# Sliding-window attention in key blocks of 64: both products of the attention on smaller tiles of the array

## The chip, the cores and the metric

The kernel runs on one NeuronCore of a Trainium2 chip. The metric is device time in microseconds from the start to the end of one execution; lower is better. The core has a matrix engine (TensorE, PE in the profile), a vector engine (VectorE, DVE), an activation engine (ScalarE, ACT), a general engine (GpSimd, POOL), and a queue engine that issues DMA transfers (SyncE, SP). Matmuls write to PSUM, which the kernel uses as eight banks of 128 partitions by 512 float32 columns. [...]

## The reference

One layer on x of 2048 tokens by 576 features, all in bfloat16:

```
xn = layernorm(x)
q, k, v = split(xn @ wqkv)           # 32 heads of 18
p = softmax(q k^T / sqrt(18)), masked to 0 <= query - key < 256
s = (p v) @ wo
h = sigmoid(xn @ w_gate) * (xn @ w_up)      # 4608 wide
out = x + s * silu(h @ w_down)
```

A query sees its own key and the 255 before it. In blocks of 128 keys, a block of 128 queries meets three key blocks, the first and last of which are cut by a triangular mask. In blocks of 64 it meets five, of which the first and the last are cut.

## The kernel before

The 2048 tokens go through in four chunks of 512 (`NCH` = 4, variable `c`). For each chunk the program builds, in this order: layer norm; the projections to q, k and v (`project`, L451); the attention; the projection by `wo` (L717); the first half of the feed-forward network, FFN1, which computes gate and up (L760), and the second half, FFN2, the product with `w_down` (L834, and L864 for the last block). Every piece of work is an `Op` with an engine, an estimated duration, dependencies and PSUM banks to choose from. `schedule` places all ops by a list scheduler with these estimates and priorities, picks the banks, and writes out one fixed program for each engine; `emit` adds the semaphore waits. At run time every engine works strictly through its program, so an instruction whose input is late holds up all that stands behind it. The order of each engine is therefore known from the code alone.

The 32 heads lie in eight groups of four (`NHG`, variable `hg`). Head j of a group lies on partitions 32j to 32j+17 of `qkp`, so the four heads of a group can be multiplied at once.

- **Scores** (`build_unit`, L568). One unit makes up to 512 score columns for each of four heads. A matmul takes 128 keys of one head as weights, on a tile of 32 rows by 128 columns of the array, and 128 to 384 queries as the moving side. The four heads sit on four row tiles and write to PSUM banks 0, 1, 2 and 3. A unit holds all four banks. Then two ACT instructions take the exponential of two banks each (L591) into one of five buffers `expr`, and DVE multiplies the triangular masks `m13` on the blocks that are cut (L623). In chunks 1 to 3 a head group has three units of 512 columns; in chunk 0 two head groups share five units, 18 key-query blocks in all.
- **p times v** (`build_pv`, L651). Weights are 128 keys by 32 columns of v with a column of ones, on tiles of 128 rows by 32 columns, one column tile for each head; the moving side is `expr`. One head group writes one bank, taken from banks 4 to 7 (FFN1 takes its banks from the same four). The op is held in `pending` and put directly ahead of a later score unit as one op (`pvsc`), so that PE goes from p times v to scores without going back to the FFN.
- **After it** (`after_pv`): DVE transposes the bank in 32 by 32 blocks (L667), takes the reciprocal of the sums (L671), scales (L675) and transposes back (L681); DMAs (L208) put the heads' rows together in `oT` for `wo`.

The list scheduler sets the scores and p times v between stretches of FFN1, whose matmuls come in pairs: gate on the upper 64 rows of the array, up on the lower 64, at the same time. `SKEW` is the number of steps by which up runs behind gate, so that in each chunk the first `SKEW` gate steps and the last `SKEW` up steps have no partner. `FB_CUTS` says where an FFN1 op may be cut to let other work in. Weights of FFN1 are streamed again in each chunk through a ring of three buffers (`RW`).

PE has four forms of tile in this program: the whole array (FFN2, warm-up, transposes of chunk 0), 64 by 128 (FFN1, q/k/v, `wo`), 32 by 128 (scores) and 128 by 32 (p times v). The scheduler's estimate adds `MODE_NS` where the form changes.

Of the kernel before, what the change touches and what calls it, by code (L numbers as in the profile page):

```python
# [5 lines left out]
ALU = mybir.AluOpType  # L6
# [42 lines left out]
SKEW = 2  # L49
# [6 lines left out]
FB_CUTS = (0, 3, 7)  # L56
LAST = 448
W_GATE = 2

# [108 lines left out]
class Builder:  # L168
# [46 lines left out]
    def alloc_memory(self):  # L215
# [33 lines left out]
        self.m13 = sb("m13", [P, 2, P], bf16)  # L249
# [9 lines left out]
        self.psb = self.ps.bitcast(bf16)  # L259

# [4 lines left out]
    def build(self):  # L265
# [22 lines left out]
        for c in range(NCH):  # L288
# [18 lines left out]
    def build_init(self):  # L307
# [7 lines left out]
        m1 = op("POOL", 300, lambda e: e.memset(self.m13[:, :, :], 1.0), "m1", prio=1)  # L315
        m2 = op("POOL", 300, lambda e: e.affine_select(
            self.m13[:, 0, :], self.m13[:, 0, :], pattern=[[1, P]], compare_op=ALU.is_ge, fill=0.0,
            base=0, channel_multiplier=-1), "m2", deps=[m1], prio=1)
        self.op_mask = op("POOL", 300, lambda e: e.affine_select(
            self.m13[:, 1, :], self.m13[:, 1, :], pattern=[[-1, P]], compare_op=ALU.is_ge, fill=0.0,  # L320
            base=-1, channel_multiplier=1), "m3", deps=[m2], prio=1)
# [208 lines left out]
    def attn_steps(self, c):  # L530
        kb0 = c * QPC
        steps = []
        if c == 0:
            for a in range(0, NHG, 2):
                b = a + 1
                steps += [([(a, 0, 0, 3, 0), (a, 3, 3, 1, 3)], True), ([(a, 1, 1, 3, 0), (b, 3, 3, 1, 3)], False),
                          ([(a, 2, 2, 2, 0), (b, 2, 2, 2, 2)], False), (a, None), ([(b, 0, 0, 3, 0)], False),
                          ([(b, 1, 1, 3, 0)], True), (b, None)]
        else:
            for a in range(NHG):  # L540
                steps += [([(a, kb0, 0, 3, 0), (a, kb0 - 2, 0, 1, 3)], False),
                          ([(a, kb0 + 2, 2, 2, 0), (a, kb0 - 1, 0, 2, 2)], True),
                          ([(a, kb0 + 1, 1, 3, 0), (a, kb0 + 3, 3, 1, 3)], False), (a, None)]
        return steps

    def build_attn(self, c):
        self.where, self.masks, self.exps = {}, {}, {}
        for u, (what, merge) in enumerate(self.attn_steps(c)):
            if merge is None:
                self.build_pv(c, what)  # L550
            else:
                self.build_unit(c, u, what, merge)

    def build_unit(self, c, u, pieces, merge):
        kb0 = c * QPC
        where = self.where
        nblk = max(pos + n for (_, _, _, n, pos) in pieces)
        hgs = sorted({p[0] for p in pieces})
        es, de = self.r_exp.take()
        ps = Psum((0, 1, 2, 3))  # L560

        def f_sc(e):
            for hg, kb, q0, n, pos in pieces:
                for j in range(4):
                    r0 = 32 * j
                    b = ps.banks[j] * 512 + pos * P
                    k0 = CH + (kb - kb0) * P if kb >= kb0 else 2 * CH + (kb - kb0 + 2) * P
                    r = e.matmul(self.ps[:, b:b + n * P],  # L568
                                 self.qkp[r0:r0 + DH, hg, k0:k0 + P],
                                 self.qkp[r0:r0 + DH, hg, q0 * P:(q0 + n) * P],  # L570
                                 start=True, stop=True, tile_position=(r0, 0))
            return r
        deps = de + [self.op_tail[hg] for hg in hgs]
        for _, kb, q0, n, pos in pieces:
            deps += self.op_q[q0:q0 + n] + ([self.op_k[kb - kb0]] if kb >= kb0 else [])
        pend = self.pending if merge else None
        if pend:
            self.pending = None
            o = self.pe(pend[1] + MODE_NS + nblk * P / 2.4 + 30, lambda e, a=pend[0], b=f_sc: (a(e), b(e))[1],
                        f"pvsc:{c}:{hgs[0]}:{u}", deps=pend[2] + deps, prio=0, psum=[pend[3], ps], mode=("c32", "r32"))  # L580
            pend[4](o)
        else:
            o = self.pe(nblk * P / 2.4 + 30, f_sc, f"sc:{c}:{hgs[0]}:{u}", deps=deps, prio=1, psum=[ps], mode="r32")
# [3 lines left out]
        for pr in range(2):  # L587
            def f_ex(e, pr=pr):
                b = ps.banks[0] * 512
                src = self.ps[:, b:b + 2048].rearrange("p (b c) -> p b c", b=4)[:, 2 * pr:2 * pr + 2, 0:nblk * P]  # L590
                return e.activation(self.expr[:, es, 2 * pr:2 * pr + 2, 0:nblk * P], src, ACTF.Exp, scale=SM_SCALE)  # L591
            exps.append(self.rd("ACT", act_ns(2 * nblk * P), f_ex, f"ex:{c}:{hgs[0]}:{u}:{pr}", deps=[o], prio=1, psum=[ps]))
        spec = {}
        for hg, kb, q0, n, pos in pieces:
            for i in range(n):
                qi = q0 + i
                where[(hg, kb, qi)] = (es, pos + i)
                dlt = kb0 + qi - kb
                if dlt == 0:
                    spec[pos + i] = 0  # L600
# [542 lines left out]
```

## Time and profile before

| | before |
|---|---|
| median of 3 runs | 575.86 us (575.33 to 576.46) |
| profiled execution, span | 574.0 us |
| median less span | 1.9 us |
| mean granted TensorE clock | 0.999 |
| PE busy | 566.3 us, 99% |
| DVE busy | 293.9 us, 51% |
| ACT busy | 303.0 us, 53% |
| scores (L568), matmuls | 704 |
| p times v (L651), matmuls | 704 |

The span runs from the first to the last instruction of the profiled execution; its device time beyond the span is not given separately, and the difference to the median of the runs stands in for it. In the profile, L568 is line 568 of the kernel, `18*128 18x384` in a row of PE is a tile with 18 rows of weights by 128 columns and 384 moving columns, and PEld is the loading of weights, which the profile lists beside the matmuls. The ends of matmuls are modelled, so two rows of PE can overlap by their lengths; the starts are measured, and it is from start to start that durations on PE are read below. Releasers in brackets say what ended an idle time.

### The profile page before, as it was taken

To read this page: it belongs to the slowest core of one execution; us is meant where nothing else is said; L and a number is where in the kernel's file an instruction comes from. 1 tells how busy PE (TensorE), PEld (TensorE's weight loads), DVE (VectorE), ACT (ScalarE), POOL (GpSimd) and SP (SyncE) were. 2 spreads that over 40 slices of the span, in tenths; PEclk is the share of its full clock that TensorE was granted. 3 is DMA by queue.
4 is the path that set the end of the run, shared out by engine and by line. 5 is a ranking of instruction groups with operands and counts; after the bars stand their busy time and mean duration, and the time that the engine had idled before them with its cause. 6 is when DMAs were issued, how large, how long until landed. Compare 5 with 4: busy or idle time off the path is not lost.

```text
span 574.0 us, 14808 instructions
## 1 busy us (share of the span) xinstructions
PE 566.3 (99%) x6350; PEld 273.6 (48%) x6350; DVE 293.9 (51%) x589; ACT 303.0 (53%) x404; POOL 23.4 (4%) x51
## 2 busy tenths in 40 slices
PE   8999999999999999999999999999999999999996
PEld 5634443457444444455753444344654444444554
DVE  5147877422247886622115888672122676774112
ACT  7456777214448887420307787760242778872201
POOL 3001110000001100000000011000000000000000
PEclk9999999999999999999999999999999999999999
DMA  8999999436936665341893666414479356651010
GB/s 206 216 197 242 224 228 228 84 68 117 203 74 136 144 157 126 82 84 42 138 220 79 146 140 150 109 46 99 56 137 185 84 124 136 136 126 41 1 40 22
DMA packets 124861, 72.82 MB, mean 127 GB/s; under 512 B 53630, under 2 KB 124286, under 8 KB 124798
## 3 DMA queue, kind: packets, MB, share of 16 engines
q1 hardware_dynamic: 124798, 71.90, 58.5%
q8 instruction: 50, 0.82, 0.7%
q14 instruction: 13, 0.11, 0.1%
HBM read 55.22 MB, written 2.36 MB: 100 GB/s over the span
## 4 chain that ended last, share of the span: by engine, by line
PE 95%; SPq 2%; DMA 2%; issue 0%; DVE 0%; ACT 0%
PE ps L760 50%; PE ps L834 23%; PE ps L451 8%; PE ps L568 5%; PE ps L651 4%; PE ps L717 3%; SPq L208 2%; PE ps L864 2%; DMA wqkv_sb<-in_A_wqkv_dram 1%; DMA wgs<-in_B_w_up_dram 1%; DVE thf L897 0%; ACT thf L895 0%; DVE thf L899 0%; DVE xf L901 0%
## 5 line engine op out<-in xcount | busy, mean ns | idle before, releaser
L760 PE MATMUL ps<-xn,wgs 64*128 64x512 bf16 x2592 | 298.2, 377 | 1.2 <-DMA wgs<-in_B_w_up_dram 1.2
L591 ACT ACTIVATE expr<-ps 128x1024 bf16<-128x1024 f32 (+1 forms) x184 | 174.9, 1003 | 45.2 <-PE ps L568 45.2
L760 PEld LDWEIGHTS ps<-xn,wgs 64*128 64x128 bf16 x2592 | 118.6, 94 | 153.4 <-issue 18.7
L834 PE MATMUL ps<-wd_sb,hT 128*128 128x512 bf16 (+1 forms) x1080 | 135.0, 286 | 0.0
L746 ACT ACTIVATE tring<-ps 128x512 bf16<-128x512 f32 x144 | 86.3, 600 | 61.7 <-PE ps L760 60.3
L623 DVE TENSOR_TENSOR expr<-expr,m 128x1024 bf16<-128x1024 bf16 (+1 forms) x152 | 81.9, 572 | 67.8 <-ACT expr L591 67.7
L750 DVE SCALAR_TENSOR_TENSOR hT<-tring,ps 128x512 bf16<-128x512 bf16 x144 | 97.1, 675 | 35.3 <-ACT tring L746 28.6
L834 PEld LDWEIGHTS ps<-wd_sb,hT 128*128 128x128 bf16 x1080 | 68.0, 98 | 66.3 <-issue 3.1
L895 ACT ACTIVATE thf<-ps 128x576 bf16<-128x576 f32 (+2 forms) x17 | 10.6, 623 | 110.6 <-PE ps L834 102.8
L897 DVE SCALAR_TENSOR_TENSOR thf<-thf,ps 128x576 bf16<-128x576 bf16 (+2 forms) x17 | 12.2, 719 | 89.5 <-ACT thf L895 89.4
L451 PE MATMUL ps<-wqkv_sb,xn 64*128 64x288 bf16 x864 | 54.7, 283 | 0.4 <-ACT xn L440 0.3
L451 PEld LDWEIGHTS ps<-wqkv_sb,xn 64*128 64x128 bf16 x864 | 42.7, 94 | 11.5 <-issue 1.6
L568 PE MATMUL ps<-qkp 18*128 18x128 bf16 (+2 forms) x704 | 36.1, 275 | 0.0
L667 DVE STREAM_TRANSPOSE tf<-ps 128x512 f32<-128x512 f32 x32 | 22.8, 714 | 12.4 <-PE ps L568 10.9
L568 PEld LDWEIGHTS ps<-qkp 18*128 18x128 bf16 x704 | 10.8, 92 | 33.4 <-issue 20.3
L499 DVE CAST pk<-ps 128x576 bf16<-128x576 f32 x15 | 11.3, 756 | 27.8 <-PE ps L451 27.8
L651 PE MATMUL ps<-expr,vau 128*32 128x256 bf16 (+2 forms) x704 | 25.6, 277 | 0.0
L633 POOL COPY qkp<-qkp 128x256 bf16<-128x256 bf16 x24 | 11.6, 485 | 315.0 <-PE ps L568 315.0
L681 DVE STREAM_TRANSPOSE op__63<-pk 128x512 bf16<-128x512 bf16 x32 | 22.7, 709 | 1.1 <-DVE pk L675 0.2
L651 PEld LDWEIGHTS ps<-expr,vau 128*32 128x32 bf16 x704 | 13.1, 96 | 15.3 <-ACT tring L746 6.8
L717 PE MATMUL ps<-wo_sb,oT 64*128 64x512 bf16 (+1 forms) x288 | 19.2, 283 | 0.0
L500 ACT ACTIVATE pk<-ps 128x576 bf16<-128x576 f32 x12 | 7.8, 652 | 18.6 <-PE ps L451 18.6
(42 smaller groups left out, 148.6 us busy)
## 6 DMA issues: line engine op xcount, KB each, us to landing
wgs<-in_B_w_gate_dram SPq DMA_DIRECT2D x48, 240.0 KB, 3.8
wgs<-in_B_w_up_dram SPq DMA_DIRECT2D x48, 240.0 KB, 4.8
wgs<-in_B_w_up_dram SPq DMA_DIRECT2D x48, 192.0 KB, 4.1
wgs<-in_B_w_gate_dram SPq DMA_DIRECT2D x48, 192.0 KB, 4.7
wd_sb<-in_B_w_down_dram SPq DMA_DIRECT2D x9, 576.0 KB, 5.9
xf<-in_A_x_dram SPq DMA_DIRECT2D x18, 144.0 KB, 2.3
out_dram<-xf SPq DMA_DIRECT2D x15, 144.0 KB, 1.8
xr<-in_A_x_dram SPq DMA_DIRECT2D x14, 144.0 KB, 4.2
```

The lines of the kernel that those rows point to most:

```text
L451: r = e.matmul(self.bank(ps, HV, hf), self.xn[r0:r0 + 64, k, i * P:(i + 1) * P], self.wqkv_sb[r0:r0 + 64, j, k, :], start=(k == 0), stop=( ...
L568: r = e.matmul(self.ps[:, b:b + n * P], self.qkp[r0:r0 + DH, hg, k0:k0 + P], self.qkp[r0:r0 + DH, hg, q0 * P:(q0 + n) * P], start=True, st ...
L591: return e.activation(self.expr[:, es, 2 * pr:2 * pr + 2, 0:nblk * P], src, ACTF.Exp, scale=SM_SCALE)
L623: return e.tensor_tensor(ap, ap, m, ALU.mult)
L651: r = e.matmul(self.ps[32 * j:32 * j + 32, b + q0 * P:b + (q0 + n) * P], vf[:, v0:v0 + 32], self.expr[:, es, j, pos * P:(pos + n) * P], st ...
L667: t1 = self.rd("DVE", dve_ns(CH), lambda e, ps=ps: e.transpose(tf.rearrange("p g d -> p (g d)"), self.bank(ps)), f"t1:{c}:{hg}", deps=[o_p ...
L681: t2 = self.op("DVE", dve_ns(CH), lambda e, on=on: e.transpose(self.op_[:, hg % NOT, :], on.rearrange("p g d -> p (g d)")), f"t2:{c}:{hg}" ...
L717: r = e.matmul(self.bank(ps2[w], n1 - n0, n), self.oT[r0:r0 + 64, kt, qi * P:(qi + 1) * P], self.wo_sb[r0:r0 + 64, kt, n0:n1], start=(swap ...
L746: return e.activation(self.tring[:, st_, :], self.bank(ps), ACTF.Tanh, scale=0.5)
L750: return e.scalar_tensor_tensor(self.hT[:, ft, :], self.tring[:, st_, :], 1.0, self.bank(ps), ALU.add, ALU.mult)
L760: return e.matmul(self.bank((pg, pu)[gu][ft]), self.wgs[r0:r0 + 64, slots[ft // FG], i, fl * P:(fl + 1) * P], self.xn[r0:r0 + 64, i, :], s ...
L834: r = e.matmul(self.ps[:, b + n0:b + n1], lhsT, self.wd_sb[:, q, fl, n0:n1], start=(ft == 0), stop=(ft == NFT - 1))
```

## The change

The attention is cut into key blocks of 64 in place of 128.

- **Scores.** A matmul takes 64 keys as weights on a tile of 32 rows by 64 columns. Even key blocks go to the lower 64 output partitions and odd ones to the upper 64 (`low` and `up` in `build_unit`), so eight tiles are in the array. A unit is always 512 columns wide; `slots` orders its pieces by length, and the two halves of a unit may have pieces of unequal length. Two head groups together have five units in chunks 1 to 3 (one of them shared, `half`) and four in chunk 0. The matmuls of the scores go from 704 to 1472.
- **p times v.** The weights are 64 keys by 32 columns, on tiles of 64 rows by 32 columns; the upper and the lower half of the array take the odd and the even key blocks and sum into different banks. One op does two head groups and holds four banks, which are now banks 0 to 3 (`PVB`), the ones that the scores use. `pending` and `pvsc` are gone. The matmuls of p times v go from 704 to 1440.
- **After it.** For each head group DVE transposes two banks (`t1`, `t3`) and adds them (`ad`). Two of the three buffers `pk` serve as room for this; POOL sets them to zero again once in each chunk (`pkz`), before the next chunk's projections are written there.
- **Masks** of 64 by 64 (`m64`) on blocks of 64, 152 multiplications of mostly 512 columns.
- `SKEW` goes from 2 to 3, `FB_CUTS` to steps of three, and the last FFN2 block of chunks 0 to 2 may also take banks 4 to 7 (`F2B`).

```diff
-SKEW = 2
+SKEW = 3
...
-FB_CUTS = (0, 3, 7)
+FB_CUTS = (0,3,6)
...
+F2B = ((0, 1), (2, 3), (6, 7), (4, 5))
+PVB = ((0,), (1,), (2,), (3,))
...
+        self.pkf = self.pk.bitcast(f32)
...
+            self.op_pkz = [self.op("POOL", 2000, lambda e: e.memset(self.pk[:, 1:RPK, :, :], 0.0), f"pkz:{c}",
+                                   deps=self.op_on[c], prio=1)]
...
+        for a in range(0, NHG, 2):
+            b = a + 1
+            if c == 0:
+                for h in (a, b):
+                    steps += [("unit", [(h, 4, 4, 1, 0), (h, 0, 0, 5, 1), (h, 6, 6, 2, 6)],
+                               [(h, 1, 0, 6, 0), (h, 7, 7, 1, 7), (h, 7, 7, 1, 6)],
+                               [(0, P, 1, 5, 0), (0, P, 0, 6, (0,)), (64, P, 0, None, None)]),
+                              ("unit", [(h, 2, 2, 5, 0), (h, 4, 5, 3, 5)], [(h, 3, 3, 5, 0), (h, 5, 5, 3, 5)],
+                               [(0, P, 0, 4, 0), (64, P, 5, None, 0)])]
+                steps += [("pv", a)]
+                continue
+            half = [("unit", [(a, 4, 4, 4, 0), (b, 4, 4, 4, 4)], [(a, -1, 0, 4, 0), (b, -1, 0, 4, 4)],
+                     [(0, 64, 0, 4, (0,)), (64, P, 3, 7, (1,))])]
+            for h in (a, b):
+                steps += [("unit", [(h, 0, 0, 5, 0), (h, -2, 0, 3, 5)], [(h, 3, 3, 5, 0), (h, 5, 5, 3, 5)],
+                           [(0, P, 0, 4, 0), (0, P, 5, 7, 2)]),
+                          ("unit", [(h, 2, 2, 5, 0), (h, 6, 6, 2, 5), (h, -4, 0, 1, 7)],
+                           [(h, 1, 1, 5, 0), (h, 7, 7, 1, 5), (h, -3, 0, 2, 6)],
+                           [(0, P, 0, 4, 0), (0, P, 5, 7, 0)])] + half
+                half = []
+            steps += [("pv", a)]
...
+        slots = sorted(((-max(p[3] for p in low[k:k + 1] + up[k:k + 1]), k) for k in range(max(len(low), len(up)))))
 
         def f_sc(e):
-            for hg, kb, q0, n, pos in pieces:
+            for _, k in slots:
                 for j in range(4):
                     r0 = 32 * j
-                    b = ps.banks[j] * 512 + pos * P
-                    k0 = CH + (kb - kb0) * P if kb >= kb0 else 2 * CH + (kb - kb0 + 2) * P
-                    r = e.matmul(self.ps[:, b:b + n * P],
-                                 self.qkp[r0:r0 + DH, hg, k0:k0 + P],
-                                 self.qkp[r0:r0 + DH, hg, q0 * P:(q0 + n) * P],
-                                 start=True, stop=True, tile_position=(r0, 0))
+                    for half, pieces in enumerate((low, up)):
+                        if k >= len(pieces):
+                            continue
+                        hg, kb, q0, n, pos = pieces[k]
+                        b = ps.banks[j] * 512 + pos * 64
+                        k0 = CH + kb * 64 if kb >= 0 else 2 * CH + (kb + 4) * 64
+                        r = e.matmul(self.ps[64 * half:64 * half + 64, b:b + n * 64],
+                                     self.qkp[r0:r0 + DH, hg, k0:k0 + 64],
+                                     self.qkp[r0:r0 + DH, hg, q0 * 64:(q0 + n) * 64],
+                                     start=True, stop=True, tile_position=(r0, 64 * half))
             return r
...
+            self.runs.setdefault(hg, ([], []))[kb % 2].append((kb, q0, n, es, pos))
+        ns = 512 / 2.4 + 30
+        o = self.pe(ns, f_sc, f"sc:{c}:{hgs[0]}:{u}", deps=deps, prio=1, psum=[ps], mode="r32")
...
+        for p0, p1, pa, pb, kind in masks:
...
+            exps.append(self.op("DVE", dve_ns(512 if pb is not None else 256, 2.0), f_mk,
+                                f"mk:{c}:{hgs[0]}:{u}:{pa}", deps=(exps if kind is None else ex) + self.op_mask, prio=1))
...
-        ps = Psum((4,), (5,), (6,), (7,), *(((0,), (1,), (2,), (3,)) if hg == NHG - 1 else ()))
+        ps2 = {hg: [Psum(*PVB) for _ in range(2)] for hg in pair}
...
+        runs = {hg: [sorted(dict(((r[0], r[1]), r) for r in side).values(), key=lambda r: -r[2])
+                     for side in self.runs[hg]] for hg in pair}
+        ncol = sum(64 * max(sum(r[2] for r in side) for side in runs[hg]) for hg in pair)
+        used = sorted({r[3] for hg in pair for side in runs[hg] for r in side})
         def f_pv(e):
+            for hg in pair:
+                for m in range(max(len(side) for side in runs[hg])):
+                    for j in range(4):
+                        v0 = (hg * 4 + j) * (DH + 1)
+                        for half, side in enumerate(runs[hg]):
+                            if m >= len(side):
+                                continue
+                            kb, q0, n, es, pos = side[m]
+                            b = ps2[hg][half].banks[0] * 512
+                            p0 = 64 * half
+                            vf = self.vau[p0:p0 + 64, (kb0 + kb // 2) % NVB, :, :].rearrange("p h d -> p (h d)")
+                            r = e.matmul(self.ps[32 * j:32 * j + 32, b + q0 * 64:b + (q0 + n) * 64],
+                                         vf[:, v0:v0 + 32], self.expr[p0:p0 + 64, es, j, pos * 64:(pos + n) * 64],
+                                         start=(m == 0), stop=(m == len(side) - 1), tile_position=(p0, 32 * j),
+                                         skip_group_check=True)
             return r
-        self.pending = (f_pv, ncol / 2.4 + 30, deps, ps, lambda o: self.after_pv(c, hg, ps, o, used))
-        if hg == NHG - 1:
-            o = self.pe(ncol / 2.4 + 30, f_pv, f"pv:{c}:{hg}", deps=deps, prio=0, psum=[ps], mode="c32")
-            self.pending[4](o)
-            self.pending = None
...
+        o = self.pe(ncol / 2.4 + 30, f_pv, f"pv:{c}:{a}", deps=self.masks[a] + self.masks[a + 1] + vdeps, prio=0,
+                    psum=ps2[a] + ps2[a + 1], mode="c32")
+        for es in used:
+            self.r_exp.release(es, o)
+        mul = None
+        pkf = [self.pkf[:, k, :, :].rearrange("p h d -> p (h d)") for k in (1, 2)]
+        bufs = {a: (self.tf[:, :, :, :].rearrange("p a b d -> p (a b d)"), pkf[1]), a + 1: (pkf[0], pkf[1])}
+        ads = []
+        qk = self.op_q + self.op_k
+        for hg in pair:
+            tf, tg = bufs[hg]
+            t1 = self.rd("DVE", dve_ns(CH), lambda e, tf=tf, hg=hg: e.transpose(tf, self.bank(ps2[hg][0])),
+                         f"t1:{c}:{hg}", deps=[o, self.last_mul] + qk, prio=3, psum=ps2[hg][:1])
+            t3 = self.rd("DVE", dve_ns(CH), lambda e, tg=tg, hg=hg: e.transpose(tg, self.bank(ps2[hg][1])),
+                         f"t3:{c}:{hg}", deps=[o, self.last_mul] + qk + ads, prio=3, psum=ps2[hg][1:])
+            tf, tg = (t.rearrange("p (g d) -> p g d", d=32)[:, :, 0:DH + 1] for t in (tf, tg))
+            ads = [self.op("DVE", dve_ns(16 * (DH + 1)), lambda e, tf=tf, tg=tg: e.tensor_tensor(tf, tf, tg, ALU.add),
+                           f"ad:{c}:{hg}", deps=[t1, t3], prio=3)]
+            bufs[hg] = (tf, ads[0])
+        for hg in pair:
+            self.after_pv(c, hg, o, *bufs[hg])
...
-        on = self.pk[:, hg % RPK, (hg // RPK % 2) * 16:(hg // RPK % 2) * 16 + 16, :]
-        prev = self.op_on[c][hg - 2 * RPK] if hg >= 2 * RPK else None
+                     deps=[ad] + dr, prio=1)
+        on = self.pk[:, 0, hg % 2 * 16:hg % 2 * 16 + 16, :]
...
-            cands = ((0, 1), (2, 3)) if blocks[-1] == QPC - 1 else ((6, 7), (4, 5), (0, 1), (2, 3))
+            cands = F2B if blocks[-1] == QPC - 1 else ((6, 7), (4, 5), (0, 1), (2, 3))
```

More of the change, by code (lines that the diff above doesn't have):

```diff
@@ L589, in f_ex @@
                 b = ps.banks[0] * 512
[L590 to L600, printed above, removed]
-                elif dlt == 2:
-                    spec[pos + i] = 1
@@ L603, in build_unit @@
[L603 to L622 removed]
+                src = self.ps[:, b:b + 2048].rearrange("p (b c) -> p b c", b=4)[:, 2 * pr:2 * pr + 2, :]
```

136 lines of the change are left out of this document (47 added, 89 removed).

## The prediction

> **What bounds the kernel now.** I read the page first, for the busy time and the chain that ended last.
>
> ```profile
> span 574.0 us, 14808 instructions
> PE 566.3 (99%) x6350; PEld 273.6 (48%) x6350; DVE 293.9 (51%) x589; ACT 303.0 (53%) x404; POOL 23.4 (4%) x51
> PE 95%; SPq 2%; DMA 2%; issue 0%; DVE 0%; ACT 0%
> PE ps L760 50%; PE ps L834 23%; PE ps L451 8%; PE ps L568 5%; PE ps L651 4%; PE ps L717 3%; SPq L208 2%; PE ps L864 2%; DMA wqkv_sb<-in_A_wqkv_dram 1%; DMA wgs<-in_B_w_up_dram 1%; DVE thf L897 0%; ACT thf L895 0%; DVE thf L899 0%; DVE xf L901 0%
> ```
>
> PE carries 95% of the chain, and the attention's two lines (L568, L651) are 9% of the span on it. The waits of PE say whether it is really never held up.
>
> ```profile
> engine line waited for: us in total, times, longest us
> PE ps L760 <- DMA wgs<-in_B_w_up_dram: 1.2, 1, 1.2
> ```
>
> After its start PE waits once, 1.2 us in chunk 0. So a change of the attention is worth what it does to PE's own time, plus any wait it brings. PE's own time I took from the order in time, from start to start:
>
> ```profile
> start us, us, engine line op out<-in xcount [idle before <-releaser]
> 221.69 0.40 PE L568 MATMUL ps<-qkp 18*128 18x384 bf16 x8
> 222.02 2.76 PE L760 MATMUL ps<-xn,wgs 64*128 64x512 bf16 x24
> 224.72 0.40 PE L568 MATMUL ps<-qkp 18*128 18x384 bf16 x8
> 225.05 2.98 PE L760 MATMUL ps<-xn,wgs 64*128 64x512 bf16 x26
> 227.96 0.84 PE L651 MATMUL ps<-expr,vau 128*32 128x384 bf16 x24
> 228.73 0.40 PE L568 MATMUL ps<-qkp 18*128 18x256 bf16 x8
> 229.06 2.55 PE L760 MATMUL ps<-xn,wgs 64*128 64x512 bf16 x22
> ...
> 62.76 0.34 PE L568 MATMUL ps<-qkp 18*128 18x384 bf16 x4
> 63.03 2.98 PE L760 MATMUL ps<-xn,wgs 64*128 64x512 bf16 x26
> 65.94 0.67 PE L651 MATMUL ps<-expr,vau 128*32 128x384 bf16 x16
> 66.55 0.34 PE L568 MATMUL ps<-qkp 18*128 18x384 bf16 x4
> ...
> 162.51 2.11 PE L760 MATMUL ps<-xn,wgs 64*128 64x512 bf16 x16
> 164.56 0.40 PE L568 MATMUL ps<-qkp 18*128 18x384 bf16 x8
> ```
>
> From these rows come three prices.
> - FFN1: 26 matmuls take 2.91 us, 24 take 2.70, so 0.108 each, and 0.11 remains at the end of each stretch (2.70 - 24 x 0.108). Between forms of tile PE therefore loses about 0.11 us.
> - p times v: 1536 columns per tile take 0.77 us, the 1152 of chunk 0 take 0.61. That is 0.42 ns a column and 0.12 fixed. Scores: 512 columns 0.33, 384 columns 0.27, so 0.47 ns and 0.09. I use 0.43 ns a column, and 0.11 us for each change of form.
> - An FFN1 step without its partner: 16 matmuls, the first two alone, took 2.05 us, where 16 x 0.108 + 0.11 is 1.84. So 0.105 more for each.
>
> That several tiles do run at once shows in a window of 16 ns after the start of a unit and of a p times v:
>
> ```profile
> 221.69 0.34 PE L568 MATMUL ps<-qkp 18*128 18x384 bf16 x4
> 227.96 0.35 PE L651 MATMUL ps<-expr,vau 128*32 128x384 bf16 x4
> ```
>
> Four matmuls start within 16 ns, some 4 ns apart, on four row tiles as on four column tiles.
>
> **The change on PE, part by part.**
>
> *Columns.* Before: 45 blocks of 128 by 128 for each of eight groups, 46,080 columns for scores and as many for p times v. After, with eight tiles at once: in chunks 1 to 3 a pair of groups has three units of 512. Its other two units have pieces of 5, 2|1 and 1|2 blocks. PE starts matmuls in the order written, so I take each slot by its longer half, 5+2+2 = 9 blocks, 576 columns; that makes 2688 for the pair, 12 pairs. In chunk 0 a group has one unit of 512 and one with slots 1|6, 5|1, 2|1, which is 13 blocks or 832 columns and not 512; 2688 for a pair again, 4 pairs. Scores: 43,008. p times v: 20 blocks a group in chunks 1 to 3 (the halves match slot for slot), 17 in chunk 0: 12 x 2560 + 4 x 2176 = 39,424. Together 82,432 for 92,160: 9728 fewer x 0.43 ns = -4.2 us.
>
> *Changes of form.* Counted in the instruction order of PE, which is fixed without a run: 240 before, 206 after. 96 stretches of attention with 28 inner steps from p times v to scores become 92 stretches without; the cuts between FFN2 and 64-row work go from 20 to 22. -34 x 0.11 = -3.7 us.
>
> *SKEW.* One more step at each end of FFN1 is alone, in four chunks: 8 x 0.108 = +0.9 us.
>
> *Starting eight tiles.* At 4 ns each the last of eight starts 14 ns later than the last of four, and the drain waits for it: 92 stretches x 14 ns = +1.3 us.
>
> *Loading weights.* No row shows 64-column weights on eight tiles. Low end 0: the fixed prices of p times v (32-column weights, 0.12) and of scores (128 columns, 0.09) hardly differ, so width does not show. High end: one whole load at the start of each stretch. A load is recorded with under 0.1 us:
>
> ```profile
> L568 PEld LDWEIGHTS ps<-qkp 18*128 18x128 bf16 x704 | 10.8, 92 | 33.4 <-issue 20.3 <-ACT expr L591 7.2 <-ACT tring L746 5.9
> L591 ACT ACTIVATE expr<-ps 128x1024 bf16<-128x1024 f32 x168 | 162.8, 1021 | 41.9 <-PE ps L568 41.9
> L623 DVE TENSOR_TENSOR expr<-expr,m 128x512 bf16<-128x512 bf16 x64 | 26.5, 419 | 3.1 <-ACT expr L591 3.1
> ```
>
> 92 x 0.092 = 8.5 us. The trace lies near the low end; I take +1.0.
>
> [...]
>
> **What runs beside PE.** ACT loses work: 184 exponentials become 152 of 1.02 us. DVE gains 32 transposes and 32 additions and loses mask time (152 multiplications of mostly 512 columns at 0.42, 64 us for 87). In chunk 2 its load was
>
> ```profile
> core 0: us, PE busy (x) PEld busy (x) DVE busy (x) ACT busy (x) POOL busy (x), PEclk, DMA share, GB/s
> 300.00:384.00 84.00, 84.00 (x1006) 34.31 (x1006) 62.36 (x126) 63.90 (x82) 5.65 (x12) 1.00 0.51 118
> ```
>
> 74%, so there is room on average. What matters is one place: scores and p times v now share banks 0 to 3, so the first unit after a p times v waits for all four transposes. DVE's order there (pairs 1 and 3 of chunks 1 to 3) is transpose, transpose, FFN product, addition, transpose, reciprocal, product, scaling, transpose. Prices from start to start:
>
> ```profile
> 346.02 0.68 DVE L750 SCALAR_TENSOR_TENSOR hT<-tring,ps 128x512 bf16<-128x512 bf16 x1
> 346.62 0.71 DVE L667 STREAM_TRANSPOSE tf<-ps 128x512 f32<-128x512 f32 x1
> 347.25 0.17 DVE L398 BATCH_NORM_AGGREGATE mv<-bnst 128x2 f32<-128x12 f32 x1
> 347.36 0.25 DVE L671 RECIPROCAL rrec<-tf 128x16 f32<-128x16 f32 x1
> 347.53 0.10 DVE L401 TENSOR_SCALAR veps<-mv 128x1 f32<-128x1 f32 x1
> 347.65 0.46 DVE L675 TENSOR_TENSOR pk<-tf,rrec 128x288 bf16<-128x288 f32 x1
> 348.14 0.71 DVE L681 STREAM_TRANSPOSE op__63<-pk 128x512 bf16<-128x512 bf16 x1
> ```
>
> Three transposes at 0.63 and the last in full 0.71, two products at 0.60, reciprocal 0.17, scaling 0.49, addition about 0.47 (nearest row: scaling, 288 elements for 304): 4.9 us, some 5.1 with the signals. PE has 48 FFN1 matmuls there, 48 x 0.108 + 0.11 = 5.3. With pair 2 it is 42 (4.6 us), and reciprocal and last transpose come earlier, 4.0. In chunk 0 the third gap is 36 (4.0 us), about even. The cover is thin but there: +0.5 us for waits. If PE runs ahead of it, the next score unit is late, and the FFN1 behind it in the queue.
>
> ```profile
> 343.11 1.93 ACT L591 ACTIVATE expr<-ps 128x1024 bf16<-128x1024 f32 x2
> ```
>
> Ahead of p times v nothing gets worse: from its last unit PE has 30 FFN1 matmuls (3.3 us and the unit's 0.37), and the two exponentials (1.93), two masks and the signals need some 3.4.
>
> At the end of a chunk p times v now comes after the last FFN1, eight FFN2 matmuls into it, so the DMAs to `oT` meet the transposes of the next chunk's xn on SP:
>
> ```profile
> 248.49 11.56 SPq L207 DMA_TRANSPOSE xn<-xnr  x8
> 252.80 17.82 PE L834 MATMUL ps<-wd_sb,hT 128*128 128x512 bf16 x144
> 520.29 4.15 SPq L208 DMA_DIRECT2D oT<-op__63  x6
> ```
>
> DVE needs some 7 to 10 us for the pair (its xn normalisations stand in between), SP 11.6 + 4.2 plus two earlier transfers of 0.7 and the waits, about 19 us from the end of FFN1. PE has FFN2's 17.7 us, p times v 1.2, then the projections, whose first six read the first two token blocks, transposed ahead of that. Nothing waits. In chunk 3 `wo` stands 136 FFN2 matmuls (17 us) behind p times v; 6.1 us of DVE and 4.2 of SP leave over 6 for the landing. `pkz` on POOL is done in the same shadow. Without it a late xn would stop PE outright.
>
> **Sum.** 574.0 - 4.2 - 3.7 + 0.9 + 1.3 + 1.0 + 0.5 = 569.8 us span; with the 1.9 us by which the median exceeds the span, 571.7.
>
> **Rivals.**
> 1. *Eight tiles do not run at once*: the two halves of a row group take turns, or PE cannot start matmuls faster than it does per matmul now. For it: no row shows row and column tiles together. Against it: the two rows of four starts in 16 ns, one of them of four tiles over the same 128 rows. Both column sums come once more, 82,432 x 0.43 = 35 us: 607.
>    [...]
> 2. *Slower by the shared banks.* DVE comes to the transposes with FFN products and masks ahead of it, and PE stands at the first unit after p times v, in 11 places (the first gap of chunk 0, 72 matmuls, is wide). It becomes slower from 0.48 us for each on average (571.7 to 577.0, by 11). With two products late (1.2 us) less margins of 0.2, 0.6 and 0, six waits of 1.0, four of 0.6 and one of 1.2 make 9.6: 581. For it: margins of 0.2. Against: DVE at 74% and no such wait of PE on DVE today.
> 3. *Weights uncovered* at each stretch, the high end: +8.5 for +1.0, 579.
> 4. *More gain*: skew, weights and waits cost nothing: 568.9.
>
> **How the numbers follow.** My forecast 66%, with a range of its own from 569.5 to 573.5; rival 4 6%; rival 2 10%; rival 3 8%; rival 1 5%; a mixture of costs that ends near no change 5%. 0.2% (1.15 us) is about what a measurement of this kernel can tell from no change. Faster 72%, same 5%, slower 23%. The range from 568.5 to 579.0 takes in rival 4, most of 3 and of the mixtures, and leaves out 1, and 2 in its larger half.
>
> **What would show it.** Score units of 0.34 and 0.37 us (0.48 in chunk 0's uneven one), p times v of 1.23 and 1.06, FFN1 stretches of 24 at 2.70 as now: right on columns and form. Units of 0.55 and p times v over 2 would be rival 1. PE waits with DVE L674 or L676 as releaser, ahead of scores, would be rival 2. Equal surplus on every unit, whatever its columns, would be rival 3 or the skew. Waits of PE on xn at a chunk's start would prove the shadow wrong.

## The result and the profile after

The changed kernel takes 571.13 us (median of 4 runs, 570.73 to 572.08), beside 576.0 us for the kernel before in the same measurement: ratio 0.9918, 95% interval 0.9904 to 0.9932. The forecast was 571.7 us, in a range from 568.5 to 579.0. The profiled execution has a span of 569.0 us, 5.0 less than before; the forecast's sum was 569.8.

From the page of the changed kernel: span, busy time, the chain that ended last, and the waits of PE.

```profile
span 569.0 us, 17867 instructions
PE 560.6 (99%) x7854; PEld 284.3 (50%) x7854; DVE 304.8 (54%) x664; ACT 274.7 (48%) x372; POOL 28.2 (5%) x55
PE 94%; SPq 2%; DMA 2%; issue 0%; ACT 0%; DVE 0%; DVEq 0%
PE ps L777 50%; PE ps L851 23%; PE ps L460 8%; PE ps L589 5%; PE ps L658 3%; PE ps L734 3%; SPq L210 2%; PE ps L881 2%; DMA wqkv_sb<-in_A_wqkv_dram 1%; DMA wgs<-in_B_w_up_dram 1%; ACT expr L509 0%; DVE xf L918 0%; DVE thf L914 0%; ACT thf L912 0%; DVE thf L916 0%
```

```profile
engine line waited for: us in total, times, longest us
PE ps L342 <- DVE neghalf L313: 1.5, 1, 1.5
PE ps L777 <- DMA wgs<-in_B_w_up_dram: 1.1, 1, 1.1
PE ps L460 <- DMA wqkv_sb<-in_A_wqkv_dram: 0.6, 2, 0.4
```

PE still carries the chain. It waits for DMAs near the start, as before, and nowhere in the attention for DVE or ACT (the 1.5 us for `neghalf` is the first wait of the program and stands in both kernels), though DVE's busy time is 11 us more and it has 75 more instructions. PE executes 1504 more matmuls in less time. In the order in time, the first pair of head groups of chunk 1 (scores are L589, p times v L658, FFN1 L777):

```profile
start us, us, engine line op out<-in xcount [idle before <-releaser]
162.36 0.42 PE L589 MATMUL ps<-qkp 18*64 18x320 bf16 x16
162.71 2.77 PE L777 MATMUL ps<-xn,wgs 64*128 64x512 bf16 x24
165.41 0.43 PE L589 MATMUL ps<-qkp 18*64 18x320 bf16 x24
165.77 2.77 PE L777 MATMUL ps<-xn,wgs 64*128 64x512 bf16 x24
...
174.93 3.41 PE L777 MATMUL ps<-xn,wgs 64*128 64x512 bf16 x30
178.27 1.35 PE L658 MATMUL ps<-expr,vau 64*32 64x320 bf16 x96
179.56 0.39 PE L777 MATMUL ps<-xn,wgs 64*128 64x512 bf16 x2
```

Read from start to start: a score unit takes 0.36 us, with 16 matmuls as with 24; a p times v of two head groups takes 1.29 us; 24 FFN1 matmuls still take 2.70. Before, the same pair of head groups took six units of 0.33 and two p times v of 0.77, 3.5 us; now five units and one p times v take 3.1. Over the whole run the score stretches come to 27.3 us (44 of 0.357 and 32 of 0.362) in place of 29.9, and p times v to 19.7 (12 of 1.29, 4 of 1.05) in place of 23.4: 6.3 us less. SKEW, the start and the end take part of that back, as below.

### The profile page after: what moved, and what is told of

Its sections match the earlier page's. It is cut to its first block, busy times and chain, and to the rows that moved or that the text cites. A ratio compares the mean times of both kernels' runs of the same rounds, so it can differ in the third digit from the quotient of the medians.

```text
span 569.0 us, 17867 instructions
## 1 busy us (share of the span) xinstructions
PE 560.6 (99%) x7854; PEld 284.3 (50%) x7854; DVE 304.8 (54%) x664; ACT 274.7 (48%) x372; POOL 28.2 (5%) x55
## 4 chain that ended last, share of the span: by engine, by line
PE 94%; SPq 2%; DMA 2%; issue 0%; ACT 0%; DVE 0%; DVEq 0%
PE ps L777 50%; PE ps L851 23%; PE ps L460 8%; PE ps L589 5%; PE ps L658 3%; PE ps L734 3%; SPq L210 2%; PE ps L881 2%; DMA wqkv_sb<-in_A_wqkv_dram 1%; DMA wgs<-in_B_w_up_dram 1%; ACT expr L509 0%; DVE xf L918 0%; DVE thf L914 0%; ACT thf L912 0%; DVE thf L916 0%
## 5 line engine op out<-in xcount | busy, mean ns | idle before, releaser
L777 PE MATMUL ps<-xn,wgs 64*128 64x512 bf16 x2592 | 298.8, 377 | 1.2 <-DMA wgs<-in_B_w_up_dram 1.1
L777 PEld LDWEIGHTS ps<-xn,wgs 64*128 64x128 bf16 x2592 | 120.8, 94 | 146.1 <-issue 9.8
L607 ACT ACTIVATE expr<-ps 128x1024 bf16<-128x1024 f32 x152 | 147.2, 1022 | 28.2 <-PE ps L589 28.2
L625 DVE TENSOR_TENSOR expr<-expr,m 128x512 bf16<-128x512 bf16 (+2 forms) x152 | 58.3, 412 | 61.8 <-ACT expr L607 61.0
L589 PE MATMUL ps<-qkp 18*64 18x320 bf16 (+4 forms) x1472 | 32.4, 259 | 0.0
L589 PEld LDWEIGHTS ps<-qkp 18*64 18x64 bf16 x1472 | 16.1, 103 | 32.5 <-issue 15.7
L636 POOL COPY qkp<-qkp 128x256 bf16<-128x256 bf16 x24 | 9.6, 398 | 248.6 <-PE ps L589 248.6
L676 DVE STREAM_TRANSPOSE pk<-ps 128x512 f32<-128x512 f32 x32 | 21.6, 675 | 0.0
L658 PEld LDWEIGHTS ps<-expr,vau 64*32 64x32 bf16 x1440 | 17.9, 92 | 6.4 <-issue 5.6
L658 PE MATMUL ps<-expr,vau 64*32 64x320 bf16 (+5 forms) x1440 | 20.7, 253 | 0.0
L674 DVE STREAM_TRANSPOSE tf<-ps 128x512 f32<-128x512 f32 x16 | 11.4, 713 | 15.4 <-PE ps L658 15.1
## 6 DMA issues: line engine op xcount, KB each, us to landing
wd_sb<-in_B_w_down_dram SPq DMA_DIRECT2D x9, 576.0 KB, 6.3
```

The costliest lines, as they stand in the source:

```text
L589: r = e.matmul(self.ps[64 * half:64 * half + 64, b:b + n * 64], self.qkp[r0:r0 + DH, hg, k0:k0 + 64], self.qkp[r0:r0 + DH, hg, q0 * 64:(q0 ...
L607: return e.activation(self.expr[:, es, 2 * pr:2 * pr + 2, :], src, ACTF.Exp, scale=SM_SCALE)
L625: return e.tensor_tensor(ap, ap, m, ALU.mult)
L658: r = e.matmul(self.ps[32 * j:32 * j + 32, b + q0 * 64:b + (q0 + n) * 64], vf[:, v0:v0 + 32], self.expr[p0:p0 + 64, es, j, pos * 64:(pos + ...
L676: t3 = self.rd("DVE", dve_ns(CH), lambda e, tg=tg, hg=hg: e.transpose(tg, self.bank(ps2[hg][1])), f"t3:{c}:{hg}", deps=[o, self.last_mul] ...
L777: return e.matmul(self.bank((pg, pu)[gu][ft]), self.wgs[r0:r0 + 64, slots[ft // FG], i, fl * P:(fl + 1) * P], self.xn[r0:r0 + 64, i, :], s ...
```

## The experiments

Three of the sum's steps were open. Do pieces of unequal length hold each other up on eight tiles, as I had priced them? Is the cover of the transposes as thin as it looked? And what do SKEW, the merging of ops and the choice of banks cost by themselves? In every run the whole reference is computed.

**The order of the matmuls on eight tiles.** The sum had taken each slot of a score unit by its longer half, because PE would start matmuls in the order written. The uneven unit of chunk 0 was to take 0.48 us by that. In the changed kernel it takes 0.36:

```profile
39.76 0.43 PE L589 MATMUL ps<-qkp 18*64 18x64 bf16 x24
40.12 1.47 PE L777 MATMUL ps<-xn,wgs 64*128 64x512 bf16 x12
```

The matmuls that had started by 39.94, 0.18 us into this unit, grouped by shape:

```profile
L589 PE MATMUL ps<-qkp 18*64 18x384 bf16 x4 | 0.4, 345 | 0.0
L589 PE MATMUL ps<-qkp 18*64 18x320 bf16 x4 | 0.3, 297 | 0.0
L589 PE MATMUL ps<-qkp 18*64 18x64 bf16 x4 | 0.2, 212 | 0.0
```

These are the first slot (1 block below, 6 above) and the lower pieces of the second (5 blocks), for all four heads. Written between those lower pieces stand the upper ones of the second slot, which wait for the six blocks; the trace has them start at 39.945 and after. So three heads' lower pieces passed an upper one that was written ahead of them. To see how far that goes, all lower pieces were written ahead of all upper ones:

```diff
-            for _, k in slots:
-                for j in range(4):
-                    r0 = 32 * j
-                    for half, pieces in enumerate((low, up)):
-                        if k >= len(pieces):
-                            continue
+            for half, pieces in enumerate((low, up)):
+                for _, k in slots:
+                    if k >= len(pieces):
+                        continue
+                    for j in range(4):
+                        r0 = 32 * j
```

> Scores of the changed kernel with all matmuls of the lower output half written ahead of those of the upper half. Theory A, tiles are independent (a matmul that waits for its own tile does not hold back one for another tile): units stay at 0.36 to 0.38 us, span within 1 us of 569.0. Rival, matmuls start strictly in the order written: the upper half starts only after the last piece of the lower half has, a unit of slots 5 and 3 takes 13 blocks for 8 (0.36 to 0.49 us), one of three slots 15 (0.55 us), 44 x 0.135 + 32 x 0.19 = 12 us, span 581.

Span 570.5; a single execution, 572.66 us beside 576.14 for before (median of 11). The same two units:

```profile
162.67 0.44 PE L589 MATMUL ps<-qkp 18*64 18x320 bf16 x16
163.04 2.76 PE L777 MATMUL ps<-xn,wgs 64*128 64x512 bf16 x24
165.74 0.46 PE L589 MATMUL ps<-qkp 18*64 18x320 bf16 x24
166.12 2.55 PE L777 MATMUL ps<-xn,wgs 64*128 64x512 bf16 x22
```

0.37 and 0.38 us, 13 and 26 ns more, 44 x 13 + 32 x 26 ns = 1.4 us in all; strict order asked for 0.49 and 0.55. The span is 0.5 us above what theory A allowed, and its mechanism stands: in these units a matmul that waited for its own tile did not hold back one for the other half of the array. In the changed kernel a score unit costs its longer half in all, 512 columns (0.36 us, the uneven unit too), and not the sum over slots of the longer piece (0.48 for the uneven unit).

**What makes p times v 0.06 us dearer than priced.** 2560 columns at 0.43 ns, the fixed 0.11 and 0.014 for eight tiles make 1.23 us; it takes 1.29. The starts of the 96 matmuls of one p times v, read from the trace in ns from the first, show where (each row is a group of eight tiles, first and last start):

```
first head group    5 blocks   0 ..  23     second head group    5 blocks  579 ..  637
                    5        146 .. 170                          5         714 ..  781
                    4        282 .. 305                          4         849 ..  917
                    3        391 .. 415                          3         957 .. 1026
                    2        474 .. 497                          2, 1     1039 .. 1165
                    1        530 .. 553
```

In the first head group eight tiles start within 23 ns, 3.3 ns apart. From the short pieces on they start 8 ns apart, 58 to 69 ns for eight. At 0.42 ns a column a group of one or two blocks lasts 27 or 53 ns, less than that. If this is the cause, short pieces should be set between long ones:

```diff
-                for m in range(max(len(side) for side in runs[hg])):
+                nm = max(len(side) for side in runs[hg])
+                for m in ((0, 5, 1, 4, 2, 3) if nm == 6 else (0, 4, 1, 3, 2)):
...
-                                         start=(m == 0), stop=(m == len(side) - 1), tile_position=(p0, 32 * j),
+                                         start=(m == 0), stop=(m == (3 if nm == 6 else 2)), tile_position=(p0, 32 * j),
```

> p times v of the changed kernel with long and short pieces alternating (5,1,5,2,4,3 blocks) in place of falling length. Theory S, PE runs short of fed instructions where short pieces come one after the other: p times v falls from 1.286 to about 1.23 us and from 1.048 to about 1.01, 12 x 0.06 + 4 x 0.04 = 0.9 us, span 568.1, ratio to before 0.990. Rival, the surplus belongs to the second head group itself (its weights, its banks): stays at 1.286, span 569.0.

570.25 us (569.86 to 570.57), ratio to before 0.9896 (0.9882 to 0.9911); span 567.7. The p times v of the rows above, in this kernel:

```profile
177.65 1.30 PE L659 MATMUL ps<-expr,vau 64*32 64x320 bf16 x96
178.88 1.47 PE L778 MATMUL ps<-xn,wgs 64*128 64x512 bf16 x12
```

1.23 us, and 1.00 in chunk 0: as theory S has it. The second head group keeps its matmuls and its banks, so the surplus did not belong to it. The weight loads of a p times v come 8.4 ns apart here too once it is under way; with a long piece beside a short one this no longer shows in its time. Whether feeding of instructions or the way of the weights sets the 8.4 ns, these runs do not separate. By the rows the new order gains 12 x 0.053 + 4 x 0.045 = 0.8 us. The span is 1.3 us shorter than that of the changed kernel, but 0.4 of this is there ahead of the first p times v (52.12 for 52.56), where the order of PE is the same, and is no effect of the edit. This is the fastest kernel of the case; its interval still overlaps that of the changed kernel.

**The cover of the transposes.** In the changed kernel the last of the four transposes ends 0.55 to 0.6 us ahead of the next score unit where 48 FFN1 matmuls stand between. DVE's order there, chunk 1:

```profile
179.71 0.72 DVE L674 STREAM_TRANSPOSE tf<-ps 128x512 f32<-128x512 f32 x1 [1.27 <-PE ps L658]
180.35 0.67 DVE L676 STREAM_TRANSPOSE pk<-ps 128x512 f32<-128x512 f32 x1
180.95 0.65 DVE L767 SCALAR_TENSOR_TENSOR hT<-tring,ps 128x512 bf16<-128x512 bf16 x1
181.52 0.46 DVE L679 TENSOR_TENSOR tf<-tf,pk 128x304 f32<-128x304 f32 x1
181.90 0.70 DVE L674 STREAM_TRANSPOSE pk<-ps 128x512 f32<-128x512 f32 x1
182.53 0.21 DVE L688 RECIPROCAL rrec<-tf 128x16 f32<-128x16 f32 x1
182.66 0.63 DVE L767 SCALAR_TENSOR_TENSOR hT<-tring,ps 128x512 bf16<-128x512 bf16 x1
183.21 0.44 DVE L692 TENSOR_TENSOR pk<-tf,rrec 128x288 bf16<-128x288 f32 x1
183.57 0.71 DVE L676 STREAM_TRANSPOSE pk<-ps 128x512 f32<-128x512 f32 x1
```

The last ends at 184.27, the score unit starts at 184.84. Two kernels put one and two further transposes (0.63 us each, into a buffer that is overwritten next) ahead of the second one; PE's order stays the same but for one gap of chunk 0, 42 in place of 36. DVE's order changes too, as shown below:

```diff
+            if hg == a:
+                dl = t1
+                for _ in range(1):          # 2 in the second kernel
+                    dl = self.rd("DVE", 1, lambda e, hg=hg: e.transpose(pkf[0], self.bank(ps2[hg][0])),
+                                 f"dl:{c}:{hg}", deps=[dl], prio=-9, psum=ps2[hg][:1])
+                    dl.lat = 0.0
+                    dls = [dl]
```

> One more transpose (0.63 us) on VectorE ahead of the second bank's, after each p times v; it writes what the next one overwrites. In the changed kernel the last transpose ends 0.55 to 0.6 us ahead of the next scores in six places, 0.65 to 0.76 in four, 0.09 in one. Theory, the shared banks are covered by these margins: 6 x 0.1 + 0.5 = about 1 us slower than the changed kernel, span 570.0. Rival, the transposes are already on PE's path (each ns of them costs): 11 x 0.63 = 7 us, span 576.

> Two more transposes (1.27 us) in the same place. Theory of margins: six waits of 0.7 to 0.75, three of 0.6, and 0.5, 0.4 and 1.2 in chunk 0, 8.4 us in all, span 577.4, so slower than before the change by some 0.6%. Rival, something else than these margins hides it (a further buffer): span within 1 us of late1.

One more: 572.09 us, ratio to before 0.9927 (0.9913 to 0.9941), 1.0 above the changed kernel, with intervals that overlap. Two more: 580.26 us, ratio 1.0066 (1.0049 to 1.0083), 9.1 above it, span 578.1. With two, PE's waits are

```profile
PE ps L784 <- DVE hT L774: 2.1, 10, 0.3
PE ps L589 <- DVE pk L683: 2.1, 6, 0.4
```

and the six stretches of 48 FFN1 matmuls grow from 5.28 to 5.92 to 6.00 us. With one, these six stay at 5.28. That is not because a whole transpose had room. In both kernels the scheduler also moved the scaling, which in the changed kernel stands ahead of the fourth transpose, behind it; with one further transpose:

```profile
185.41 0.65 DVE L683 STREAM_TRANSPOSE pk<-ps 128x512 f32<-128x512 f32 x1
185.99 0.41 DVE L699 TENSOR_TENSOR pk<-tf,rrec 128x288 bf16<-128x288 f32 x1
```

So the first added transpose came with 0.36 us of scaling taken away, and the fourth ends only some 0.4 us later after its p times v than in the changed kernel; in the six stretches, 0.56 to 0.61 us ahead of the scores became 0.18 to 0.31. Where PE does wait (two transposes more), the scores start 0.145 us after the fourth transpose has ended, so 0.57 us ahead means some 0.42 free, and 0.18 means almost nothing. The second added transpose moves the fourth one by some 0.75 us more and makes each of these stretches 0.63 to 0.71 longer. Over all twelve gaps between a p times v and the next scores the two add 8.8 us. Half of the recorded waits are not ahead of scores (L589) but ahead of FFN1 (L784), for its product hT: this stands behind the transposes on DVE, so FFN1's banks come free late. Rival 2 of the prediction thus exists, at a price near the one that it was given (9.6 us), and the change has 0.4 us of margin against it in these six places. In the gap of 72 matmuls in chunk 0, which the prediction called wide, the fourth transpose ends 0.09 us ahead of the scores, because DVE puts layer norm and FFN1 products ahead of it; two more transposes lengthen this gap by 0.9 us.

**SKEW and the cuts alone.** Each of the two settings was put into the other kernel.

```diff
-SKEW = 3
+SKEW = 2
-FB_CUTS = (0,3,6)
+FB_CUTS = (0, 3, 7)
```

> The changed kernel with SKEW and FB_CUTS as before the change (2 and 0,3,7). 206 changes of form as in the changed kernel. Theory, SKEW 3 costs two lone FFN1 steps more in each chunk, 8 x 0.108 us: 0.9 us faster than the changed kernel, span 568.1, ratio to before 0.990. Rival, the cuts at every third step are what lets the attention in on time, and with uneven cuts PE waits for the transposes or exponentials: no faster or slower, with PE waits ahead of scores (L589) in the trace.

> The kernel before with SKEW 3 and cuts at every third step, nothing else of the change. 240 changes of form as before. Theory: 8 x 0.108 = 0.9 us slower than before, span 574.9, ratio 1.0015. Rival, the cuts bring a gain of their own: ratio under 1.

Before with SKEW 3: 577.37 us, ratio 1.0022 (1.0011 to 1.0032), so it costs 1.3 us (0.6 to 1.8), with 0.9 worked out. The changed kernel with SKEW 2: 571.27 us, ratio 0.992 (0.9901 to 0.9939), no gain. Its profile has the gain at the lone steps: the first and the last FFN1 stretch of each of chunks 1 to 3 take 0.21 us more than 0.108 for each matmul and 0.11 for the change of form, where the changed kernel has 0.31 to 0.32. It loses 0.9 us in chunk 0, where one stretch of 46 takes 5.99 us in place of 5.07. Beyond that at the program's start PE's waits in this profile are

```profile
PE ps L777 <- ACT expr L607: 0.6, 1, 0.6
PE ps L777 <- DMA wgs<-in_B_w_up_dram: 0.4, 1, 0.4
```

The second lies in that stretch, behind its first 18 matmuls, and is one for weights; the first is at a place where the changed kernel waits 1.1 us. So neither theory is the whole of it: the lone steps cost what was priced, and in this profile a wait for weights, not for transposes or exponentials, takes the gain back. That the cuts at every third step avoid this wait is not shown: the order of chunk 0 differs as a whole, and the runs of this kernel spread from 570.1 to 574.05 us. The two settings together were tried on the kernel with mixed pieces:

> The changed kernel with long and short pieces of p times v alternating and with SKEW 2. If both gains hold side by side: 0.9 us of pvmix and 0.9 us of SKEW, span 567.2 or with pvmix's own span 566.8, ratio to before 0.988.

571.61 us, ratio 0.9929 (0.9906 to 0.9952), with runs from 570.67 to 575.28. A miss: not faster than mixed pieces alone. Its profiled run is the longest of them, with a wait of 2.9 us behind the same 18 matmuls, and then 3.41 us (102.33 to 105.74) at a granted clock of 0.50, which costs half of them:

```profile
PE ps L778 <- DMA wgs<-in_B_w_up_dram: 4.1, 2, 2.9
```

FFN1 of chunk 0 waits for its weights by an amount that differs from profile to profile (0.4 us with SKEW 2, 1.1 in the changed kernel, 4.1 here), and here PE meets that stream at a second place. Even the fastest run (570.67 us) is not below mixed pieces alone, and why is not shown.

**The merged op alone.** The kernel before with p times v not put ahead of scores:

```diff
-        pend = self.pending if merge else None
+        pend = None
...
-        if hg == NHG - 1:
+        if True:
```

> The kernel before with p times v as an op of its own, not put directly ahead of scores; same matmuls, 265 changes of form for 240. Theory, each costs 0.11 us: 25 x 0.11 = 2.8 us slower than before, span 576.8, ratio 1.005. Rival, the changes of form hide behind something and only columns count: ratio 1.000.

583.52 us, ratio 1.0123 (1.0108 to 1.0138): 7.6 us slower in place of 2.8. The price of a change of form is the same as in the forecast, 0.11 us (8 FFN1 matmuls ahead of a p times v take 0.97 us, 8 x 0.108 + 0.11). The rest is not that price. The scheduler put a fourth score unit of chunk 1 into FFN2 of chunk 0, where before it has three, and around it a stretch of 0.33 us takes 2.59 and the 72 FFN2 matmuls behind it 1.7 us too long:

```profile
PE ps L834 <- ACT expr L591: 2.2, 1, 2.2
```

The granted clock accounts for the last: 1.0 us behind that wait it fell to 0.50 for 3.41 us, and half of 3.41 is 1.7:

```profile
157.18 10.67 PE L834 MATMUL ps<-wd_sb,hT 128*128 128x512 bf16 x72 [2.20 <-ACT expr L591]
158.21:161.62 3.41, 3.41 (x17) 1.45 (x16) 0.00 (x0) 0.00 (x0) 0.00 (x0) 0.50 1.06 212
```

The 4.8 us that are left over are thus, within 0.1, 2.3 in that stretch (2.59 less 0.33), 1.7 of half clock behind it and 0.9 of later start in this profile. The run therefore gives no clean price for a change of form; the stretches do.

**The banks alone.** p times v on banks 4 to 7, which FFN1 uses, in place of 0 to 3:

```diff
-PVB = ((0,), (1,), (2,), (3,))
+PVB = ((4,), (5,), (6,), (7,))
```

> The changed kernel with p times v on banks 4 to 7 (FFN1's) in place of 0 to 3. The scheduler then finds no four free banks while FFN1 runs, and puts three of four pairs of head groups of each chunk behind FFN1, unit after unit. Theory, it is FFN1 that hides the exponentials (about 2.45 us from one unit to the next: 0.45 to the first exponential, 1.93 for two): 15 units in each of chunks 1 to 3 and 12 in chunk 0 stand bare at 2.45 us for the 0.36 they take of PE now, 57 x 2.0 = 115 us, plus p times v waiting for masks: 680 to 700 us. Rival, the banks do not matter: 569 to 575 us.

A single execution: 763.38 us, beside 575.03 for before. With four of FFN1's banks needed at once the attention leaves FFN1's shadow, and PE waits for ACT 44 times. Of the 70 us or so beyond the expectation, 28 are PE's own: it is busy for 588.6 us in place of 560.6, and the fall of the granted clock shown here, which I had not thought of, goes with it. Another 23 are waits for DMAs of q and k (11.9) and of `oT` (11.5) that the changed kernel does not have; the rest is not assigned. Busy times and granted clock in a stretch of attention behind FFN2, and in one of FFN1:

```profile
core 0: us, PE busy (x) PEld busy (x) DVE busy (x) ACT busy (x) POOL busy (x), PEclk, DMA share, GB/s
671.00:700.00 29.00, 8.35 (x288) 4.59 (x288) 13.03 (x31) 18.07 (x19) 0.00 (x0) 0.56 0.05 11
579.00:650.00 71.00, 71.00 (x656) 41.47 (x654) 26.35 (x40) 22.52 (x38) 0.00 (x0) 1.00 0.54 122
```

In the first of these, where PE is busy 29% of the time, its mean granted clock is 0.56 (1.00 up to 674.4 us, 0.50 from there on), and a p times v takes 2.27 us for the 1.29 at full clock. The units around the fall:

```profile
671.27 0.42 PE L589 MATMUL ps<-qkp 18*64 18x320 bf16 x16 [1.62 <-DVE thf L914]
673.75 0.43 PE L589 MATMUL ps<-qkp 18*64 18x320 bf16 x24 [2.06 <-ACT expr L607]
676.38 0.65 PE L589 MATMUL ps<-qkp 18*64 18x256 bf16 x16 [2.20 <-ACT expr L607]
```

The idle times of PE ahead of the fall are 1.62 and 2.06 us, with 0.4 us of work between them. The two falls shown further up followed single waits of 2.2 and 2.9 us, while waits of 1.9 us for weights, in the kernels with one and two further transposes, were followed by none. No run here was made to find the limit.

## Why the prediction was right

**The bound.** PE carried 95% of the chain and carries 94%. That the change is worth what it does to PE's own time held: nothing that was added to DVE, POOL or SP shows on PE.

**Columns, -4.2 us: too small by 2.0.** The step that failed is "PE starts matmuls in the order written, so I take each slot by its longer half". Before the change the starts follow the written order (in the unit at 221.69 us the pieces of 384 columns start from 221.693 to 221.703, those of 128 from 221.867 to 221.876), but there each tile has both pieces, so these rows do not show whether a piece waits for one of another tile. After it, slots of the two halves did not wait for each other. All 76 units cost 512 columns and all p times v the longer half in all (20 and 16 blocks a group): 38,912 and 38,912 columns, 14,336 fewer than before, 6.2 us at the same price. The uneven unit of chunk 0 took 0.362 us and not 0.48. The 1.06 us for a p times v of chunk 0 came out as 1.05 by luck: one block too many was counted (17 for 16), and the cost of short pieces was not.

**Changes of form, -3.7 us.** The traces have 240 and 206 of them, as counted; the price stayed at 0.11 us in the rows of the changed kernel (24 FFN1 matmuls in 2.70).

**SKEW, +0.9 us.** Measured by itself as 1.3, with an interval that holds 0.9.

**Eight tiles and their weights, +1.3 and +1.0 us.** Units of the same 512 columns went from 0.330 to 0.357 us, 27 ns, where 14 + 11 had been taken. In the trace a unit's second slot starts 160 ns after its first; 5 blocks at 0.42 ns a column are 133. Before the change 174 ns stood there for 160 of columns. So 13 ns more lie at the start, beside 14 at the end, where the eighth tile comes later. If all of these 13 are the weights', which no run here separates, they cost about what was taken (11), far from the 92 ns of a whole load: 13 ns is the most that this trace leaves for them.

**Missing: +0.9 us** for the short pieces of p times v (12 x 0.06 and 4 x 0.04), which no step had. It was the first cost that the mixed order removed.

**Waits, +0.5 us: none.** The margins were wider than worked out (0.42 us net of signals for the 48, where 0.2 had been expected), because transposes that follow each other take 0.60 to 0.64 and the additions 0.38. Only three p times v lie some 0.02 to 0.04 us above the others.

With these sizes the sum is -6.2 - 3.7 + 0.9 + 2.3 + 0.9 = -5.8 us against a measured span of -5.0. Two places that no step had lie between them. The first score unit starts 0.37 later in this profile (36.70 for 36.34); over the profiles of this case that start lies between 35.97 and 37.21, so this may be chance and not the change. And the end became longer by 0.54: from the start of the last FFN2 stretch to the end of the span it is 13.51 us before and 14.05 in the changed kernel and in its variants with the same banks. DVE there adds the last 448 columns only after its work on the last 128, so the first of its two transfers to the output is issued 1.1 us later in this stretch and the second behind it:

```profile
560.52 8.98 PE L864 MATMUL ps<-wd_sb,hT 128*128 128x448 bf16 x72
569.19 0.39 DVE L901 TENSOR_TENSOR xf<-xf,thf 128x448 bf16<-128x448 bf16 x1
...
554.96 8.99 PE L881 MATMUL ps<-wd_sb,hT 128*128 128x448 bf16 x72
564.77 0.52 DVE L918 TENSOR_TENSOR xf<-xf,thf 128x448 bf16<-128x448 bf16 x2
```

These 0.9 us account for the 0.8, within the rounding of the prices. That the forecast of 571.7 came so close is in part luck: columns were 2.0 too dear and waits 0.5, p times v was 0.9 too cheap, and the 0.9 of start and end was missing.

**The rivals.** Eight tiles do run at once: their starts lie within 23 ns, and units take 0.36 us (rival 1 asked for 0.55). Weights stand uncovered for 13 ns at most and not 92 (rival 3). The shared banks (rival 2) are hidden by some 0.4 us in the six regular places, and the second added transpose shows what they cost without that. Of rival 4 (no cost for the later start of the eighth tile, for weights and for waits) only the waits came about; the further gain came from the columns, which it did not name, and was used up elsewhere.

## What to carry to other kernels

Count the longest queue of each tile, not the written order, when matmuls of unequal length share the array (here 0.36 us for an uneven unit that the written order had put at 0.48); and price a row-and-column tiling by its fixed costs (here 0.11 us for each change of form and some 27 ns a unit for eight tiles), together 0.14 of the 0.36 us of a unit. Alternate long and short pieces where many small matmuls follow each other (here 1.23 us for 1.29 in a p times v). When two stages are put on the same banks, work out the margin between the last reader and the next writer on the reader's own queue, and test it by adding work there, and see whether the order of that queue stayed the same: here 0.4 us were free, and some 0.7 us beyond that, in twelve places, cost more than the whole change brought.

## What the runs showed of the hardware

- Matmuls of the two column halves of 32 by 64 tiles started independently in the units read here: pieces written later passed pieces written earlier by 0.13 us (39.81 and 39.945, changed kernel), and even with all of one half written first the units grew by 13 to 26 ns alone (0.37 and 0.38 us for 0.36).
- In a p times v of the changed kernel (178.27 us) eight tiles start 3.3 ns apart at its head; the weight loads, and with them the starts, come some 8.4 ns apart after 43 loads; with long and short pieces mixed the loads do so after 33.
- With PE busy throughout (71.00 of 71.00 us, banks 4 to 7) the granted clock was 1.00. Single waits of PE of 2.2 us (p times v not merged) and 2.9 us (mixed pieces with SKEW 2) were each followed by 3.41 us at 0.50, single waits of 1.9 us (one and two further transposes) by none; with PE busy 29% of 29 us (banks 4 to 7) the mean was 0.56, and a bare p times v took 1.8 times as long (2.27 us for 1.29).
- The wait of FFN1 for its weights in chunk 0 was between 0.4 and 4.1 us in those profiles that show one (banks 4 to 7 aside), by itself as large as the effects of single settings.
